# The first row without w_out: gated values through DRAM, output products a row behind

## The chip, the cores and the metric

One core of a Trainium2 chip runs the program. TensorE multiplies matrices, VectorE and ScalarE do elementwise work, POOL (GpSimd) takes a share of it, and SyncE issues all the DMAs. The metric is the device time of one execution in microseconds, the median over runs.

## The reference

Eight items of x (8 heads, 512 rows of 64) and a state of 32 rows a head go through attention in both directions, and then two feed-forward blocks run over 4608 tokens of width 512:

```python
scores = scale * x @ state^T;  xread = softmax(scores) @ state       # 512 rows an item
sread = softmax(scale * state @ x^T) @ x                             # 32 rows an item
t = concat([xread, sread]) as (tokens, 512)
gate = sigmoid(t @ w_gate); val = t @ w_val                          # 512 -> 1536
y = (gate * val) @ w_out                                             # 1536 -> 512
h = y @ w_in; u = h * softmax(h); out = layernorm(u) * g @ w_out2    # 512 -> 1024 -> 512
```

All weights of the feed-forward blocks arrive as 64-bit floats.

## The kernel before

The work goes in rows, one for each item (the eight sread pieces together make one more). A row computes, for 12 column blocks c of 128 of w_gate and w_val: 12 matmuls for gate and value into gps and vps (`first_mm`), the sigmoid of gps into sg (ScalarE, L599), the product with vps into sg (VectorE, L603, called gate product here), the split of sg into a high part gh and a low part gl, and 12 matmuls that add gh and gl times the rows c of w_out into the four sums acc (`out_acc`, called output products, always one column behind). Each fp32 product is three matmuls, high x high, high x low and low x high; a split is one copy for the high part and one subtraction for the low part. xread is never formed: TensorE multiplies the state with the weights first (`state_w1` for the first row, one column at a time, L580; `state_w` for the others, half a pair of columns at a time, L516), the result is split into mh and ml (L131, L137), and `first_mm` multiplies these with the softmax weights ah and al. While row b runs, the attention of item b + 1 is spread over its columns (`parts`).

In the first row the weights are also made from their 64-bit words (class Conv). `load` issues the DMA of 512 KB into a stage, `take` is two ScalarE operations (L197, L198), `form` two bit operations and a sign step on VectorE (L205, L208, L215), `add` an integer addition on POOL (L225), which frees the stage. For w_gate and w_val that ends in wf; for w_out `split` follows (ScalarE copy and POOL subtraction, L234) into woh and wol. So the first row makes three such blocks a column, and in it gl comes from POOL (L609). In the second row `split_w` splits wf into xe and xo (ScalarE and POOL, L504), two pieces a column; the third row's states (`state_w` for item 2, with item 3) need them, six matmuls each.

Inside a row each engine runs its instructions in the order in which the code is written; SyncE issues DMAs in that order too. At the end of a row `y_spill` sends the four sums to DRAM. From the third row on, made states come partly from DRAM: item 3's are stored in msp by `state_w` and loaded by `state_load`, and later ones come from qsp.

## Time and profile before

| | us |
|---|---|
| median of three runs (1111.26 to 1114.22) | 1113.05 |
| the profiled execution | 1113.68 |
| its span | 1111.8 |
| TensorE busy | 1079.4 (97%) |
| VectorE busy | 760.7 (68%) |
| ScalarE busy | 577.1 (52%) |
| POOL busy | 383.5 (34%) |

The span is the time from the first to the last event that the profile shows. The shares are means over rows that have different limits, so the first rows have to be read apart. The profile names lines of the kernel before; the changed kernel's lines are some higher.

### The profile page before, as it was taken

What the parts mean: (1) busy time and instruction counts of PE and PEld (TensorE: products, weight loads), DVE (VectorE), ACT (ScalarE), POOL (GpSimd) and SP (SyncE); (2) the same over time, 40 slices, a digit from 0 to 9 for tenths busy, and PEclk for the clock granted to TensorE, in tenths of its full rate; (3) what the DMA queues carried; (4) which work ended last, traced back from release to release, by engine and by line L of the source; (5) the groups of instructions that cost most, each with busy time, mean ns of one, the idle gap of its engine ahead of it and who ended that gap; (6) DMA issues with size and microseconds to landing.
All of it is one profiled execution on the core that took longest, in us unless ns stands there. A gap on an engine that the chain in (4) does not pass through costs nothing.

```text
span 1111.8 us, 16156 instructions
## 1 busy us (share of the span) xinstructions
PE 1079.4 (97%) x5497; PEld 848.5 (76%) x5497; DVE 760.7 (68%) x1335; ACT 577.1 (52%) x1120; POOL 383.5 (34%) x441
## 2 busy tenths in 40 slices
PE   8877899999999999999999999999999999999998
PEld 6655567777877767778878998877788878888887
DVE  5999956367466556556365367997677777778773
ACT  5766545555444344334344344665556566565553
POOL 2777733310000000000000042216576667677551
PEclk9899999999999999999999999999999999999999
DMA  8764040241274374352341325421543543553441
GB/s 229 238 203 138 1 116 1 68 103 34 62 184 167 127 220 132 102 143 67 89 114 48 125 96 152 114 57 58 161 152 124 168 164 124 176 166 121 153 143 38
DMA packets 148946, 135.62 MB, mean 122 GB/s; under 512 B 74240, under 2 KB 114432, under 8 KB 148864
## 3 DMA queue, kind: packets, MB, share of 16 engines
q1 hardware_dynamic: 148864, 134.60, 40.6%
q8 instruction: 43, 0.70, 0.3%
q14 instruction: 39, 0.32, 0.1%
HBM read 84.74 MB, written 49.81 MB: 121 GB/s over the span
## 4 chain that ended last, share of the span: by engine, by line
PE 74%; DVE 15%; issue 3%; DMA 3%; ACT 2%; SPq 2%; POOL 1%; DVEq 0%; POOLq 0%; ACTq 0%
PE acc L140 10%; PE acc L142 9%; PE acc L141 9%; PE att L142 5%; PE att L140 5%; PE att L141 5%; PE gps L140 4%; PE gps L141 4%; PE gps L142 4%; PE vps L140 4%; PE vps L141 4%; PE vps L142 4%; DVE wf L215 2%; DVE wf L205 2%; DVE wf L208 1%
## 5 line engine op out<-in xcount | busy, mean ns | idle before, releaser
L140 PE MATMUL acc<-gh,woh 128*128 128x512 f32 (+1 forms) x432 | 172.5, 399 | 0.7 <-ACT gh L131 0.7
L141 PE MATMUL acc<-gl,woh 128*128 128x512 f32 (+1 forms) x432 | 166.1, 384 | 1.9 <-POOL gl L609 1.3
L142 PE MATMUL acc<-gh,wol 128*128 128x512 f32 (+1 forms) x432 | 165.5, 383 | 0.0
L603 DVE TENSOR_TENSOR sg<-vps,sg 128x512 f32<-128x512 f32 (+1 forms) x108 | 71.0, 658 | 137.8 <-PE vps L142 118.3
L599 ACT ACTIVATE sg<-gps 128x512 f32<-128x512 f32 (+1 forms) x108 | 61.6, 571 | 150.6 <-PE gps L142 149.0
L140 PEld LDWEIGHTS acc<-gh,woh 128*128 128x128 f32 x432 | 82.4, 191 | 42.1 <-issue 26.1
L258 POOL MEMSET xtr<- 32x256 f32 x14 | 4.2, 303 | 272.1 <-PE att L326 271.7
L141 PEld LDWEIGHTS acc<-gl,woh 128*128 128x128 f32 x432 | 82.4, 191 | 17.4 <-POOL gl L609 2.5
L142 PEld LDWEIGHTS acc<-gh,wol 128*128 128x128 f32 x432 | 82.3, 191 | 16.1
L814 POOL TENSOR_TENSOR wol<-ut,woh 128x512 fp32r<-128x512 f32 x48 | 61.8, 1302 | 90.7 <-ACT woh L131 90.7
L131 ACT ACTIVATE gh<-sg 128x512 fp32r<-128x512 f32 (+1 forms) x101 | 60.6, 600 | 62.1 <-DVE sg L603 62.1
L225 POOL TENSOR_TENSOR tt<-tt,xn 128x512 int32<-128x512 int32 x16 | 23.5, 1471 | 195.0 <-DVE tt L215 172.1
L609 DVE TENSOR_TENSOR gl<-sg,gh 128x512 fp32r<-128x512 f32 (+1 forms) x97 | 68.9, 710 | 17.9 <-ACT gh L131 14.4
L140 PE MATMUL gps<-ah,mh 128*128 128x512 f32 x192 | 76.1, 397 | 4.8 <-DVE ml L137 3.0
L142 PE MATMUL att<-woh,wol 128*128 128x512 f32 (+1 forms) x204 | 79.6, 390 | 0.7 <-POOL wol L814 0.6
L140 PE MATMUL att<-woh,woh 128*128 128x512 f32 (+1 forms) x204 | 79.8, 391 | 0.0
L141 PE MATMUL att<-wol,woh 128*128 128x512 f32 (+1 forms) x204 | 79.3, 389 | 0.0
L140 PE MATMUL vps<-ah,mh 128*128 128x512 f32 x192 | 75.2, 392 | 1.1 <-DVE ml L137 1.1
L141 PE MATMUL gps<-al,mh 128*128 128x512 f32 x192 | 75.4, 393 | 0.7 <-DVE al L137 0.7
L142 PE MATMUL gps<-ah,ml 128*128 128x512 f32 x192 | 75.4, 393 | 0.1
L142 PE MATMUL vps<-ah,ml 128*128 128x512 f32 x192 | 75.2, 392 | 0.0
L141 PE MATMUL vps<-al,mh 128*128 128x512 f32 x192 | 75.0, 391 | 0.0
(464 smaller groups left out, 2762.8 us busy)
## 6 DMA issues: line engine op xcount, KB each, us to landing
usp<-ub SPq DMA_DIRECT2D x32, 512.0 KB, 2.6
ut<-usp SPq DMA_DIRECT2D x128, 128.0 KB, 2.9
qsp<-qst SPq DMA_DIRECT2D x48, 256.0 KB, 2.3
stg<-qsp SPq DMA_DIRECT2D x192, 64.0 KB, 2.0
out_dram<-sg SPq DMA_DIRECT2D x32, 256.0 KB, 3.0
xn<-in_x_dram SPq DMA_DIRECT2D x15, 512.0 KB, 5.2
e2t<-in_x_dram SPq DMA_DIRECT2D x96, 64.0 KB, 2.5
stge<-in_moe_w_out_dram SPq DMA_DIRECT2D x10, 512.0 KB, 3.6
```

Source lines behind the costliest of these rows:

```text
L131: return act(dst, src, AF.Copy)
L140: mm(o, lh, rh, start=start, stop=False, **kw)
L141: mm(o, lh, rl, start=False, stop=False, **kw)
L142: return mm(o, ll, rh, start=False, stop=stop, **kw)
L205: vec.tensor_scalar(out=t, in0=t, scalar1=EXP_LO, scalar2=EXP_HI, op0=ALU.max, op1=ALU.min)
L208: vec.tensor_scalar(out=tu, in0=tu, scalar1=3, scalar2=0x3FFFFFFF, op0=ALU.logical_shift_left, op1=ALU.bitwise_and)
L215: vec.scalar_tensor_tensor(out=tu, in0=hi, scalar=0xC0000000, in1=tu, op0=ALU.bitwise_and, op1=ALU.bitwise_or)
L225: pool.tensor_tensor(out=ti, in0=ti, in1=lo, op=ALU.add)
L599: act(sg[c % 2][:, 0:n], gps[:, 0:n], AF.Sigmoid)
L603: vec.tensor_tensor(out=g, in0=vps[:, 0:n], in1=g, op=ALU.mult)
L609: eng.tensor_tensor(out=gl[c % 2][:, 0:n], in0=sg[c % 2][:, 0:n], in1=r(gh[c % 2][:, 0:n]), op=ALU.subtract)
L814: pool.tensor_tensor(out=lv, in0=wv[:, 4 * q:4 * q + 4], in1=r(hv), op=ALU.subtract)
```

## The change

The first row converts w_gate and w_val only. Its gated values go to DRAM (gsp[0]), column by column; it makes no output products. Instead it makes the states of the second row, from the weights in wf as they become ready, a column later, and sends them to DRAM (msp[1]). The second row loads them, splits them, converts w_out (three stages of its own), reloads the first row's gated values and makes the first row's output products; its own gated values go to DRAM too (gsp[1]). A new loop of 12 columns before the third row reloads those, makes the second row's output products and three states of the third row. The splits of wf go one a column in eight columns of the second row and two a column in eight columns of the new loop. The stages of the first row are eight instead of ten, none of them shared with the spill buffers.

```diff
--- before.py
+++ after.py
@@ -15,7 +15,7 @@
 ALU = mybir.AluOpType
 AX = mybir.AxisListType
 P = 128
-STAGES = 10
+STAGES = 8
 WARM = 11
 EXPS = 7
 QUAD = 4
@@ -104,7 +104,7 @@
 
     early = ExitStack()
     sbe = early.enter_context(tc.tile_pool(name="sbe", bufs=1, side="right"))
-    stg0 = stg + [sbe.tile([P, 1024], F32, name=f"stge{i}") for i in range(STAGES - 2)]
+    stg0 = [sbe.tile([P, 1024], F32, name=f"stge{i}") for i in range(STAGES)]
     cvt0 = [sbe.tile([P, 512], F32, name=f"cvte{i}") for i in range(4)]
     xq1 = [sbe.tile([P, S], F32, name=f"xq{i}") for i in range(4)]
     stf1 = sbe.tile([P, 512], F32, name="stf1")
@@ -117,6 +117,7 @@
     ysp = [tc.dram_tile([KC, P, S if b < B else SR], F32, name=f"ysp{b}") for b in range(B + 1)]
     ssp = tc.dram_tile([B, P, KC * NS], F32, name="ssp")
     qsp = [tc.dram_tile([H, P, 512], F32, name=f"qsp{p}") for p in range(NF1 // 2)]
+    gsp = [[tc.dram_tile([P, 512], F32, name=f"gsp{b}_{c}") for c in range(NF1)] for b in range(2)]
     msp = [tc.dram_tile([NF1, P, 512], F32, name=f"msp{b}") for b in range(B)]
 
     mm = nc.tensor.matmul
@@ -511,11 +512,7 @@
         n = 2 * p + g
         h, l = mh[i % 3], ml[i % 3]
         s = spill[n % 4]
-        if b < 2:
-            for q in range(2):
-                mm(o[64 * q:64 * q + 64, :], stt[b % 2][:, 2 * g + q, :], wpart(wf, p, 2 * g + q), start=True, stop=True)
-            put(o, h, l, hi)
-        elif b < QUAD and b % 2 == 0:
+        if b < QUAD and b % 2 == 0:
 
             for q, o in enumerate((gps, o2)):
                 k = 2 * g + q
@@ -529,6 +526,15 @@
                 nc.sync.dma_start(out=msp[b + 1][n, 64 - 64 * q:128 - 64 * q], in_=s[64 * q:64 * q + 64])
         else:
             put(s, h, l, hi)
+
+    def state_next(n, hi=hi_of):
+
+        p, g = divmod(n, 2)
+        o, s = acc[2], spill[n % 4]
+        for q in range(2):
+            mm(o[64 * q:64 * q + 64, :], stt[1][:, 2 * g + q, :], wpart(wf, p, 2 * g + q), start=True, stop=True)
+        hi(s, o)
+        nc.sync.dma_start(out=msp[1][n], in_=s)
 
     def state_load(b, n):
         if b < QUAD:
@@ -614,6 +620,17 @@
         for m in ms:
             sl = slice(m * P, (m + 1) * P)
             mm3(ps_acc(m, n), h[:, sl], l[:, sl], gh[i][:, 0:n], gl[i][:, 0:n], c == 0, c == NF1 - 1)
+
+
+    def g_store(b, c):
+        nc.sync.dma_start(out=gsp[b][c], in_=sg[c % 2])
+
+    def g_load(b, c, ring):
+        if c < NF1:
+            nc.sync.dma_start(out=ring[c % len(ring)], in_=gsp[b][c])
+
+    def g_split(c, ring, hi=hi_of):
+        put(ring[c % len(ring)], gh[c % 2], gl[c % 2], hi)
 
     def y_spill(b, n, after):
         for m, s in enumerate(xtr + e2t if after == SREAD else [tt[0], ee[0], ee[1], tt[1]]):
@@ -846,10 +863,7 @@
     def rings(n):
         return (n % 2, xn[n % 2]), tt
 
-    jobs = [job(c, t) for c in range(2) for t in range(2)]
-    for c in range(NF1):
-        jobs += [job(c, 2)] + ([job(c + 2, t) for t in range(2)] if c + 2 < NF1 else [])
-    conv = Conv(jobs, rings0)
+    conv = Conv([job(c, t) for c in range(NF1) for t in range(2)], rings0)
 
 
     ring = [(b, p, g) for b in blocks[1:] if b < B for p in range(NF1 // 2) for g in range(2)]
@@ -871,7 +885,7 @@
         loaded = max(loaded, made - NF1)
         while loaded < min(made - NF1 + n, len(ring)):
             b, p, g = ring[loaded]
-            if b < 2 or paired(b) and b % 2 == 0 or b >= QUAD and quads and quads[0] <= (p, 2 * g + 1):
+            if b < 1 or paired(b) and b % 2 == 0 or b >= QUAD and quads and quads[0] <= (p, 2 * g + 1):
                 return
             state_load(b, 2 * p + g)
             loaded += 1
@@ -993,63 +1007,99 @@
                     conv.take()
 
 
-
-        ahead = {4: 3, 5: 3, EXPS: 0}
+        ahead = {EXPS - 2: 2, EXPS - 1: 2, EXPS: 0}
         for c in range(NF1):
-            part = parts[c]
+            pe, others = parts[c]
             if c > 0:
                 first_mm(0, c, 0, 0)
             sigma(c, S)
-            if c == EXPS + 1:
-                conv.split(hi_vec)
-                gated_hi(c - 1, S, hi_vec)
-                gated_lo(c - 1, S)
-                first_mm(0, c, 1, 0)
-                form(2)
-                state_w1(c + 1, att[0])
-                take(1)
-                gated(c, S)
-                out_acc(c - 1, S)
-                form(1)
-                conv.split()
-                gated_hi(c, S)
-                gated_lo(c, S, pool)
-                take(ahead.get(c, 2))
-                part[1]()
-                continue
-            form(2)
+            form(3)
             if c > 0:
                 first_mm(0, c, 1, 0)
             else:
                 state_w1(1, acc[1])
             gated(c, S)
-            take(1)
-            if part[0]:
-                part[0]()
-            if c + 1 == NF1:
-                a_next(blocks[1])
-                make()
-                make(o=vps)
-            elif c > 0:
-                state_w1(c + 1)
+            g_store(0, c)
             if c != EXPS:
-                conv.split()
-            if c == EXPS:
-                part[1]()
+                take(1)
+            if pe:
+                pe()
+            hi = hi_vec if c == EXPS else hi_of
+            if 0 < c < NF1 - 1:
+                state_w1(c + 1, acc[1], hi=hi)
+            if c > 0:
+                state_next(c - 1, hi)
+            take(ahead.get(c, 1))
+            others()
+        state_next(NF1 - 1)
+        a_next(blocks[1])
+        loads(3)
+        make()
+        make()
+    early.close()
+    for p in range(2):
+        x_pool(p)
+    early = ExitStack()
+    sbe = early.enter_context(tc.tile_pool(name="sbe2", bufs=1, side="right"))
+    stg2 = [sbe.tile([P, 1024], F32, name=f"stgf{i}") for i in range(3)]
+    cvt2 = [sbe.tile([P, 512], F32, name=f"cvtf{i}") for i in range(2)]
+    gst = [sbe.tile([P, 512], F32, name=f"gst{i}") for i in range(3)]
+    conv = Conv([job(c, 2) for c in range(NF1)], lambda n: ((n % 3, stg2[n % 3]), cvt2))
+
+    with tc.manual_schedule():
+        parts = attention(2)
+        for _ in range(3):
+            conv.load()
+        for c in range(2):
+            g_load(0, c, gst)
+        conv.step(1)
+        for c in range(NF1):
+            pe, others = parts[c] if c < len(parts) else (None, None)
+            hi = hi_vec if others == exps else hi_of
+            first_mm(1, c, 0, used)
+            sigma(c, S)
+            first_mm(1, c, 1, used)
+            used += 2 * (c % 2)
+            gated(c, S)
+            g_store(1, c)
+            if others == exps:
+                a_cols(1)
+                exps()
+            if c == NF1 - 1:
+                a_next(2)
+            if pe:
+                pe()
+            if made - NF1 < NF1:
+                make(1, hi=hi)
             if c > 0:
                 out_acc(c - 1, S)
-            if c != EXPS:
-                gated_hi(c, S)
-            form(1)
-            if c != EXPS:
-                gated_lo(c, S, pool)
-                take(ahead.get(c, 2))
-                part[1]()
+            g_split(c, gst, hi)
+            g_load(0, c + 2, gst)
+            loads(3)
+            conv.step(1)
+            if others and others != exps:
+                others()
+            if c == 0:
+                load_xq(2, 1)
+            if 2 <= c < 10:
+                split_w(1)
+        for c in range(2):
+            g_load(1, c, sg)
+    assert not conv.jobs and not conv.loaded and not conv.joined
     early.close()
-    for p in range(3):
-        x_pool(p)
+
     with tc.manual_schedule():
-        for n_b, b in enumerate(blocks[1:], 1):
+        for c in range(NF1):
+            make(o2=vps)
+            out_acc((c - 1) % NF1, S)
+            g_split(c, sg)
+            g_load(1, c + 2, sg)
+            if c == 0:
+                y_spill(0, S, 1)
+            if c < 8:
+                split_w(2)
+    with tc.manual_schedule():
+        for n_b, b in enumerate(blocks[2:], 2):
             before = blocks[n_b - 1]
             n_before = S if before < B else SR
             n = S if b < B else SR
@@ -1124,8 +1174,6 @@
                         load_xq(n_b + 1, 1)
                 if nxt == SREAD and c == len(parts):
                     nc.sync.dma_start(out=xn[0][:, 0:KC * SR].rearrange("p (b e) -> p b e", b=B), in_=ssp.rearrange("b p e -> p b e"))
-                if n_b == 1:
-                    split_w(2)
                 if b == SREAD and c == 0:
                     conv = Conv([(rows(w_in2, k, f), win(k, f), None) for k in range(KC) for f in range(2)], rings)
                     conv.load()
```

TensorE in the first row, one column: the last product of gate and value, the states (wf is the converted weights, stt_113 and stt_114 the states of item 0 and 1), and what follows. Before:

```order
L142 MATMUL vps<-ah_90,ml 128x512
L580 MATMUL gps<-wf_145,stt_113 64x256 x4
L140 MATMUL acc_174<-gh_96,woh_68 128x512
L141 MATMUL acc_174<-gl_98,woh_68 128x512
L142 MATMUL acc_174<-gh_96,wol_80 128x512
L140 MATMUL acc_175<-gh_96,woh_68 128x512
```

And in the changed kernel:

```order
L143 MATMUL vps<-ah_90,ml 128x512
L586 MATMUL acc_175<-wf_145,stt_113 64x256 x4
L535 MATMUL acc_176<-wf_149,stt_114 64x512 x2
L141 MATMUL gps<-ah_89,mh 128x512
L142 MATMUL gps<-al_91,mh 128x512
L143 MATMUL gps<-ah_89,ml 128x512
```

The output products (acc, gh, woh) are gone from the column; four matmuls of the second row's states (L535) stand in their place, between the first row's states (L586) and the next product.

SyncE where the first row ends (ssp takes sread, xn and e2t the x of item 2, stg the spilled states). Before:

```order
L427 DMA ssp<-e2t_108 128x128
L263 DMA xn_99<-in_x_dram 128x4x256
L263 DMA xn_100<-in_x_dram 128x4x256
L280 DMA e2t_107<-in_x_dram 32x16x32 x4
L280 DMA e2t_108<-in_x_dram 32x16x32 x4
L625 DMA ysp_184<-tt_103 128x512
```

And in the changed kernel, where msp is the second row's states and gsp the gated values:

```order
L537 DMA msp_225<-stg_112 128x512
L428 DMA ssp<-e2t_108 128x128
L264 DMA xn_99<-in_x_dram 128x4x256
L264 DMA xn_100<-in_x_dram 128x4x256
L281 DMA e2t_107<-in_x_dram 32x16x32 x4
L281 DMA e2t_108<-in_x_dram 32x16x32 x4
L537 DMA msp_225<-stg_112 128x512
L541 DMA stg_111<-msp_225 128x512 x2
L541 DMA stg_112<-msp_225 128x512
L626 DMA gsp_0_212<-sg_109 128x512
```

The loads of the first three states (stg from msp) stand behind the two loads of xn, the eight of e2t and the store of the last state.

POOL in the second row (xo is the low part of wf, wol that of w_out, cvtf its 64-bit conversion). Before:

```order
L504 TENSOR_TENSOR xo_1206<-wf_153,xe_1205 128x512 x4
L504 TENSOR_TENSOR xo_1211<-wf_149,xe_1210 128x512 x4
L504 TENSOR_TENSOR xo_1216<-wf_145,xe_1215 128x512 x4
L504 TENSOR_TENSOR xo_1542<-wf_141,xe_1541 128x512 x4
L504 TENSOR_TENSOR xo_1666<-wf_137,xe_1665 128x512 x2
```

And in the changed kernel, three columns:

```order
L505 TENSOR_TENSOR xo_1025<-wf_153,xe_1024 128x512
L235 TENSOR_TENSOR wol_81<-cvtf_1037,woh_69 128x512
L226 TENSOR_TENSOR cvtf_1038<-cvtf_1038,stgf_1036 128x512
L505 TENSOR_TENSOR xo_1025<-wf_153,xe_1024 128x512
L235 TENSOR_TENSOR wol_82<-cvtf_1038,woh_70 128x512
L226 TENSOR_TENSOR cvtf_1037<-cvtf_1037,stgf_1034 128x512
L505 TENSOR_TENSOR xo_1025<-wf_153,xe_1024 128x512
L235 TENSOR_TENSOR wol_83<-cvtf_1037,woh_71 128x512
L226 TENSOR_TENSOR cvtf_1038<-cvtf_1038,stgf_1035 128x512
```

One piece of wf a column is left there, and the addition and the split of w_out have come in.

## Rows read from the trace of the kernel before

**Rows 1.** The page's 40 slices of 27.8 us: busy tenths of TensorE and VectorE.
```profile
PE   8877899999999999999999999999999999999998
...
DVE  5999956367466556556365367997677777778773
```

**Rows 2.** Windows: us, busy (instructions) PE, PEld, DVE, ACT, POOL, PEclk, DMA share, GB/s.
```profile
30.00:35.00 5.00, 3.94 (x22) 2.17 (x21) 4.97 (x9) 4.73 (x8) 3.31 (x3) 0.94 1.08 365
30.95:141.36 110.41, 91.78 (x520) 63.38 (x521) 107.78 (x158) 71.19 (x131) 81.22 (x59) 0.95 0.43 135
40.00:45.00 5.00, 5.00 (x17) 3.67 (x14) 4.96 (x9) 1.71 (x4) 3.32 (x3) 0.66 0.34 109
141.36:227.05 85.69, 85.69 (x432) 61.23 (x430) 45.90 (x77) 44.90 (x87) 30.82 (x25) 1.00 0.26 61
```

**Rows 3.** Timeline of VectorE, first row and (last) second: start us, us, line, operation, tiles.
```profile
70.49 0.41 DVE L208 TENSOR_SCALAR wf<-wf 128x512 uint32<-128x512 uint32 x1
70.82 0.68 DVE L215 SCALAR_TENSOR_TENSOR cvte<-stge,cvte 128x512 uint32<-128x512 uint32 x1
...
72.03 0.67 DVE L603 TENSOR_TENSOR sg<-vps,sg 128x512 f32<-128x512 f32 x1
...
78.40 1.50 DVE L205 TENSOR_SCALAR wf<-wf 128x512 f32<-128x512 f32 x1
...
81.69 0.68 DVE L603 TENSOR_TENSOR sg<-vps,sg 128x512 f32<-128x512 f32 x1
...
96.11 0.68 DVE L349 TENSOR_TENSOR tt<-tt,smm 128x512 f32<-128x512 f32 x1
...
97.49 0.73 DVE L205 TENSOR_SCALAR cvte<-cvte 128x512 f32<-128x512 f32 x1
...
146.57 0.69 DVE L137 TENSOR_TENSOR ml<-gps,mh 128x512 fp32r<-128x512 f32 x1 [1.53 <-ACT mh L131]
```

**Rows 4.** Timeline of POOL, first row and (last) second row.
```profile
71.63 1.63 POOL L225 TENSOR_TENSOR cvte<-cvte,stge 128x512 int32<-128x512 int32 x1 [1.69 <-DVE cvte L215]
...
78.15 1.47 POOL L609 TENSOR_TENSOR gl<-sg,gh 128x512 fp32r<-128x512 f32 x1
...
149.46 2.56 POOL L504 TENSOR_TENSOR xo<-wf,xe 128x512 fp32r<-128x512 f32 x2 [7.00 <-ACT xe L131]
```

**Rows 5.** Timeline of TensorE, after a wait in the first row, and in the second.
```profile
39.19 1.08 PE L580 MATMUL gps<-wf,stt 128*64 128x256 f32 x8 [1.95 <-POOL wf L225]
...
40.60 0.62 PE L141 MATMUL acc<-gl,woh 128*128 128x512 f32 x1
...
44.01 0.51 PE L140 MATMUL acc<-gh,woh 128*128 128x512 f32 x1
...
180.47 1.08 PE L516 MATMUL gps<-wf,stt 128*64 128x512 f32 x4
181.47 0.50 PE L140 MATMUL acc<-gh,woh 128*128 128x512 f32 x1
...
184.34 0.39 PE L140 MATMUL gps<-ah,mh 128*128 128x512 f32 x1
...
187.15 1.08 PE L516 MATMUL gps<-wf,stt 128*64 128x512 f32 x4
```

**Rows 6.** Timeline of ScalarE in the second row, the high half of a state product.
```profile
145.94 0.60 ACT L131 ACTIVATE mh<-gps 128x512 fp32r<-128x512 f32 x1 [2.36 <-PE gps L516]
```

**Rows 7.** Timeline of SyncE, issues of DMAs.
```profile
141.17 0.94 SPq L263 DMA_DIRECT2D xn<-in_x_dram  x2
142.21 5.85 SPq L280 DMA_DIRECT2D e2t<-in_x_dram  x8
...
302.44 1.31 SPq L535 DMA_DIRECT2D stg<-msp  x3
```

**Rows 8.** Instructions on the tensor msp: its transfers from issue to landing.
```profile
DMA to landing us min/median/max: 2.2/2.3/5.6
```

**Rows 9.** DMA issues by line, 15 to 40 us: KB each, median us to landing.
```profile
stg<-in_moe_w_gate_dram SPq DMA_DIRECT2D x1, 512.0 KB, 8.5
```

## The prediction

> **What bounds the kernel now.** I read the page's slices first: in the second to fifth, VectorE is at nine tenths and TensorE at seven or eight; from the sixth on TensorE is at nine [rows 1]. Then the windows, cut where the program changes rows. From 30.95 us (the weights by states for column 1) to 141.36 us (the second row's first product) VectorE works 107.8 of 110.4 us and POOL 81.2; in the second row, to 227.05 us, TensorE works all of 85.69 and VectorE 45.9 [rows 2]. So the first row is set by converting weights, and the second by TensorE.
>
> One column step of the first row shows how. Gate products stand 9.66 us apart, at 72.03 and 81.69. A bit operation issues every 0.33 us and the sign step every 0.6 [rows 3], but the one at 78.40 takes 1.50, because POOL is in an operation from 78.15 to 79.62 [rows 4]. The gate product at 72.03, which reads one operand in PSUM, runs in 0.67 beside POOL's addition of 71.63. So bit operations, and VectorE operations with both operands in SBUF, wait for POOL and POOL for them. Such work of one step: POOL 5 x 1.28 (two in 2.56) = 6.4; VectorE 3 conversions x (2 x 0.33 + 0.6) = 3.8 [rows 3, 4]; together 10.2 in a step of 9.66.
>
> The Trainium skill (SBUF — State Buffer, "SBUF: two separate sides") calls this pair of ports an exclusive lock held for the whole instruction. The step agrees nearly: 10.2 us of locked work pass in 9.66. As a mere sum, the second row after the change would hold 71.7 us of locked work by the rule and 67.8 by that ratio; both are below the 72.2 that TensorE needs there (below), which would give 1110. I go by the order of the operations instead.
>
> How much TensorE waits in the first row: a plain step of the second row is 6.68 us [rows 5]: 1.00 for four state matmuls, 2.87 for the 12 output matmuls, 2.81 for the 12 of gate and value. Attention is what is left of 85.69 - 12 x 2.81 - 12 x 2.87 - 10 x 1.00 - 2 x 1.4 (states of row three: six matmuls of 0.23) = 4.8 a row. The first row then holds 11 x 2.81 + 11 x 2.87 + 13 x 1.00 + 7.0 of attention (the next row's 4.8, and 2.2 that I estimate for the half which item 0 still owes) = 82.5 of 110.4. **The prize is 28 us**, if the rest hides.
>
> **The change, part by part.** TensorE's instructions are kept; they change places. Times count from the profiled execution's start.
>
> *First row, step by step.* The 12 conversions, splits and output products of w_out leave; four state matmuls a step for the second row come in. TensorE has 2.81 + 1.00 + 1.00 = 4.81 a step. The new chain, state matmuls to mh to ml to the next product, has to fit in the second group of state matmuls: mh takes 0.60 on ScalarE and ml starts 0.63 after it began [rows 3, 6], so the product can start 0.75 after the states end, under the 1.00. VectorE has 2 x 1.27 + gate product 0.6 + ml 0.6 + attention of some 1.3 (an estimate: 45.9 of the second row less 38 operations of 0.68, a twelfth of it, less its waits for POOL) = 5.0: level with TensorE. Column 1's product starts 2.0 after 30.95 (states 1.0, mh 0.6, and starts), at 32.9, as before. From there to column 11's: 10 x 4.81 = 48.1, attention 6.1 (0.7 comes before or after), then 2.81: the row would end at 89.9.
> What is late: columns 6 and 7 convert three weights instead of two, so ml comes 0.7 and 1.1 late. At the exponentials' column VectorE is in series: after ml the subtraction, maximum and scale 1.4 (96.11 to 97.49 before) [rows 3], six bit operations and three sign steps 3.8, 1.9 of POOL's three additions of the step before that fall on locked operations, gate product 0.6, and the high half, now on VectorE, 0.6: 8.3 against TensorE's 3.8, which ends at the first states. Product 8 starts 10.0 after product 7, 5.2 late. After an idle 1.95 us before 39.19 the granted clock is 0.66 of full from 40 to 45: eight matmuls from 40.60 to 44.01 start 0.43 apart instead of 0.23, at the lower level of 1.2 GHz [rows 2, 5]. I add 2.1 for such a restart. The first row's last product ends at 89.9 + 1.8 + 5.2 + 2.1 = **99.0** (bounds 93, if the exponentials' step goes as the others, and 108, rival one).
> The stores of gated values and states cost nothing here: 2 x 0.52 + 2 x 0.26 = 1.57 MB a step is 4.3 us at the 365 GB/s of rows 2, in a step of 4.8 to 6. The queue is a rival below.
>
> *The boundary.* Before, the second row's states came off TensorE; now they come from DRAM, and their loads stand on SyncE behind the x of row three (second piece in the section on the change). Counted from the end of the last product: spill of state 10 stored at 2.0 + 0.45, ssp 0.4, xn 0.94, eight x pieces 5.85 [rows 7]. Before, nothing that TensorE needed stood behind those eight. Then the store of state 11, 0.5 (three loads issue in 1.31, rows 7), the first load landing 2.3 after issue [rows 8], mh 0.6 and the matmul's start: 13.8 in all, of which TensorE works 2.4. Nothing else is ready for it, since output products wait for the next loop. The second row starts at **112.8** (111 if the x pieces issue at xn's 0.47 each, 116 if the load takes the 5.6 of rows 8), and at the lower clock: 2.1 more.
>
> *Second row.* TensorE loses its state matmuls: 12 x 2.81 + 11 x 2.87 + 4.8 = 70.1, + 2.1 clock = 72.2. w_out's conversion moves here. POOL: 12 splits, 11 additions, 8 splits of gate and value = 31 x 1.28 = 39.7. VectorE, locked: ml 10 x 0.6 and gl 12 x 0.6, which now read SBUF on both sides, conversions 11 x 1.27, attention about 4.8 (estimated from its subtractions and products) = 32.0. That 71.7 is level with TensorE's 72.2 is why order decides. Walking the steps with each engine's order and alternating the lock: at column 1 the scores wait for transposes that stand behind ml, gl and a conversion, 2.0; at column 3, 0.5; from column 4 on wol or gl arrives 0.4 to 1.2 after the output product could start, some 2.3 together. **77.0** (72.2 with no wait at all, 84 with two and a half times these).
>
> *The new loop.* 12 x 2.87 + three states of row three 3 x 1.4 = 38.6. Each reload of a gated value must land within two steps of 2.8: gl is done 2.4 into a step (0.6 + 0.6 and one POOL operation), issue 0.4, 2.3 to land, so 5.1 of 5.6. POOL's two splits a step (2.56) can hold gl back by one operation. I take 1.5 for this and the spill of four sums: **40.1** (38.6 to 46). It makes three states where before two were ahead, so row three is 1.4 shorter.
>
> *Unchanged or nothing:* the start to 30.95 (eight stages instead of ten: the same first six loads are issued ahead of x; w_out's were waited for by nobody there); from row three on the instructions are the same.
>
> *Sum.* 99.0 + 13.8 + 77.0 + 40.1 - 1.4 = 228.5, against 227.05: **+1.4 us**. The profiled execution took 1113.68 (span 1111.8 and 1.9 around it), the median of the runs is 1113.05. 1113.68 + 1.4 = 1115.1; I say 1115. Of the prize, the first row's own waits keep 9.6, the boundary takes 11.4 and 2.1, the second row 4.8, the loop 1.5: 29.4.
>
> **The rivals.** *One: the gated stores hold the first row (slower).* A store of gated values is issued behind two weight loads that wait for POOL's additions, some 3 us after the product, and the sigmoid two columns later writes the same buffer. By the walk it must land within about 7 us of its issue. 512 KB loads in a full queue took up to 8.5 [rows 9]; with two such loads ahead of it a store at 9 us delays gate product, ml and the next product by 2, in five of the ten steps: +10, 1125. Against it: 1.57 MB need 4.3 us of the step, so the queue should drain.
> *Two: the lock lets more pass than I walk (faster).* Locked work passed at 10.2 in 9.66; if VectorE and POOL overlap a little in every pair, the second row runs at TensorE's 72.2 (-4.8), columns 6 to 8 of the first lose 3 of their 7: -8, 1107. Against it: the 1.50 of rows 3 is a full wait.
> *Three: everything hides (faster).* Only the boundary and its clock remain, 13.5 of 28: -14.5, 1099. Against it: VectorE and TensorE are level in both rows, and no slack is left for attention's uneven steps.
>
> **How the numbers follow.** About 0.3%, or 3.3 us, is what a measurement here can tell from no change. Forecast, 0.45: faster 0.06, same 0.29, slower 0.10; its own range 1108 to 1121. Rival one, 0.25: slower 0.25. Rival two, 0.23: faster 0.20, same 0.03. Rival three, 0.07: faster. Together faster 0.33, same 0.32, slower 0.35. The range reaches into both sides, from 1102 (below it rival three) to 1126 (above it the worse half of rival one).
>
> **What would show it.** Gate products in the first row 5 to 6.5 us apart, save one of about 10; the last near 99. TensorE idle for about 10 us near 102, released by a load of states, and a lower clock after it. In the second row waits of TensorE for POOL's wol and VectorE's gl of about 1 us each, with POOL near 40 us busy; 12 steps of about 2.9 after it. Wrong if the first row's steps stay above 7 (ended by a DMA: rival one), or if TensorE is busy through the second row (rival two), or if the wait at the boundary is under 6.

## The result and the profile after

The changed kernel takes 1119.55 us (median of 1117.92 to 1120.16), the kernel before 1112.65 beside it: ratio 1.0059, interval 1.0042 to 1.0077, or 4.7 to 8.6 us slower. The forecast was +1.4 (1115.0, own range 1108 to 1121). The time lies in that range; the size of the loss does not follow from the sum, which had called it no change. The profiled execution has a span of 1118.4, 6.6 more than before.

The page's slices after the change, against [rows 1]:
```profile
PE   7976789999999999999999999999999999999998
...
DVE  6975799457556556556365367997577778778773
POOL 2541256610000000000000042216566667676551
PEclk9989899999999999999999999999999999999999
```
VectorE, full in the second to fifth slice before, is now full in the second, sixth and seventh: the second row carries w_out's conversion. TensorE has a hole in the fourth (6, from 84 to 112 us); from the seventh on it reads as before.

The windows, cut where the prediction's terms end, against [rows 2] (columns: the window and its length, busy us and instructions of PE, PEld, DVE, ACT, POOL, granted clock, DMA share, GB/s):
```profile
30.01:99.65 69.64, 62.20 (x406) 37.74 (x407) 56.75 (x114) 46.98 (x86) 32.37 (x25) 0.95 0.71 233
```
```profile
...
99.65:115.92 16.27, 2.48 (x12) 0.54 (x10) 2.59 (x6) 3.34 (x8) 0.00 (x0) 0.71 0.87 248
115.92:195.00 79.08, 73.11 (x366) 55.93 (x367) 71.63 (x104) 50.21 (x96) 43.55 (x32) 0.97 0.61 182
195.00:242.37 47.37, 46.31 (x205) 37.32 (x205) 23.03 (x30) 27.06 (x48) 24.01 (x17) 1.00 0.46 132
```
The first is the first row, from column 1's product to the end of the last; the second the boundary; the third the second row; the fourth the loop and row three up to its gate product 1 (at 237.74 before, where the same stretch, from 227.05, took 10.69). The boundary's 16.27 us with 2.48 of TensorE is the longest single loss.

| us | forecast | measured | difference |
|---|---|---|---|
| start, to column 1's product | 32.9 | 30.0 | -2.9 |
| first row | 66.1 | 69.6 | +3.5 |
| boundary | 13.8 | 16.3 | +2.5 |
| second row | 77.0 | 79.1 | +2.1 |
| loop and row three to gate product 1 (40.1 - 1.4 + 10.69) | 49.4 | 47.4 | -2.0 |
| from there to the end (874.1 before: span less 237.74) | 874.1 | 876.0 | +2.0 |

The differences sum to +5.2, which is the measured 6.6 less the forecast 1.4. Two of them are scatter: among eleven traces of the changed kernel and of its versions below that have the same code up to there, the first gate product stands between 30.57 and 36.27 us, and in two traces of the kernel before at 33.58 and 33.10; the stretch behind row three's gate product 1 varies from 873 to 877. So the first row's end (99.65) came near the forecast 99.0 by two errors that cancel: the row was 3.5 longer, and started 2.9 earlier in this execution. From gate product 0 of row one to gate product 1 of row three, which leaves both out, it is 204.2 before (204.2 again in the second trace) and 211.7 after: **+7.5**.

The boundary, first on SyncE, where the loads stand in issue order, against [rows 7]:
```profile
102.89 1.02 SPq L264 DMA_DIRECT2D xn<-in_x_dram  x2
104.01 6.28 SPq L281 DMA_DIRECT2D e2t<-in_x_dram  x8
110.38 0.43 SPq L537 DMA_DIRECT2D msp<-stg  x1
110.86 1.40 SPq L541 DMA_DIRECT2D stg<-msp  x3
```
then on ScalarE and TensorE (in brackets the idle time before and what ended it):
```profile
103.36 1.14 ACT L132 ACTIVATE ah<-ee 128x512 fp32r<-128x512 f32 x2
115.23 1.22 ACT L132 ACTIVATE mh<-stg 128x512 fp32r<-128x512 f32 x2 [10.73 <-DMA stg<-msp]
```
```profile
101.74 1.08 PE L535 MATMUL acc<-wf,stt 128*64 128x512 f32 x4 [0.70 <-ACT stg L132]
115.92 0.79 PE L141 MATMUL gps<-ah,mh 128*128 128x512 f32 x1 [13.10 <-ACT mh L132]
```
The new row's scores were split at 104.5; everything after that waits for three state loads that SyncE issues behind x. The first is used 4.4 us after its issue, where 2.3 [rows 8] was assumed. A matmul of 0.79 shows the lower clock behind the idle.

The exponentials' column on VectorE, against the 1.4 of [rows 3]:
```profile
67.18 0.68 DVE L350 TENSOR_TENSOR tt<-tt,smm 128x512 f32<-128x512 f32 x1
67.78 0.68 DVE L369 TENSOR_REDUCE st<-att 128x1 f32<-128x512 f32 x1
68.49 0.15 DVE L370 TENSOR_SCALAR st<-st 128x1 f32<-128x1 f32 x1
68.56 2.54 DVE L206 TENSOR_SCALAR wf<-wf 128x512 f32<-128x512 f32 x3
71.02 1.08 DVE L209 TENSOR_SCALAR wf<-wf 128x512 uint32<-128x512 uint32 x3
72.03 2.97 DVE L216 SCALAR_TENSOR_TENSOR wf<-stge,wf 128x512 uint32<-128x512 uint32 x3
74.92 0.68 DVE L609 TENSOR_TENSOR sg<-vps,sg 128x512 f32<-128x512 f32 x1
75.52 0.68 DVE L135 CAST mh<-acc 128x512 fp32r<-128x512 f32 x1
```
```profile
76.34 0.76 PE L141 MATMUL gps<-ah,mh 128*128 128x512 f32 x1 [4.61 <-DVE mh L135]
```
This is the forecast's series in its order: product 8 starts 10.9 after product 7 (10.0 forecast), 6.4 of it three conversions (5.7 forecast). TensorE then works at the lower level: 0.57 of full from 75 to 80.

The second row's waits of TensorE, 116 to 195 us (us in total, times, longest):
```profile
...
PE vps L141 <- DVE sg L609: 1.7, 1, 1.7
PE att L327 <- DVE xtr L323: 1.6, 1, 1.6
PE gps L143 <- DVE ml L138: 1.4, 1, 1.4
PE acc L143 <- POOL wol L235: 1.2, 2, 0.6
```
Left out is the boundary's 13.1. These sum to 5.9 against 4.8, and only 1.2 is wol's. VectorE and POOL do stand in each other's way here:
```profile
127.73 1.79 DVE L138 TENSOR_TENSOR gl<-gst,gh 128x512 fp32r<-128x512 f32 x1
```
```profile
127.47 1.50 POOL L235 TENSOR_TENSOR wol<-cvtf,woh 128x512 fp32r<-128x512 f32 x1 [0.95 <-ACT woh L132]
```
A subtraction of 0.68 takes 1.79 and ends 0.55 after POOL's, as if it had begun when POOL let go. That agrees with what the Trainium skill (SBUF — State Buffer, "SBUF: two separate sides") states of the port pair that the two share: the operation that starts first has it, as an exclusive lock, for the whole instruction.

### The profile page after: what moved, and what is told of

It reads as the page before. It is cut to its first block, busy times and chain, and to the rows that moved or that the text cites. A ratio compares the mean times of both kernels' runs of the same rounds, so it can differ in the third digit from the quotient of the medians.

```text
span 1118.4 us, 16344 instructions
## 1 busy us (share of the span) xinstructions
PE 1073.3 (96%) x5497; PEld 844.1 (75%) x5497; DVE 756.2 (68%) x1346; ACT 584.5 (52%) x1132; POOL 368.3 (33%) x430
## 4 chain that ended last, share of the span: by engine, by line
PE 68%; DVE 13%; DMA 8%; issue 4%; ACT 3%; SPq 3%; POOL 2%; DVEq 0%; POOLq 0%; ACTq 0%
PE acc L141 10%; PE acc L142 9%; PE acc L143 9%; PE att L143 4%; PE att L141 4%; PE att L142 4%; PE gps L141 4%; PE gps L143 4%; PE gps L142 4%; PE vps L141 4%; PE vps L142 3%; PE vps L143 3%; DMA usp<-ub 2%; POOL tt L226 2%; PE gps L569 1%
## 5 line engine op out<-in xcount | busy, mean ns | idle before, releaser
L141 PE MATMUL acc<-gh,woh 128*128 128x512 f32 (+1 forms) x432 | 168.9, 391 | 0.8 <-ACT gh L132 0.8
L142 PE MATMUL acc<-gl,woh 128*128 128x512 f32 (+1 forms) x432 | 163.7, 379 | 1.3 <-DVE gl L138 1.1
L141 PEld LDWEIGHTS acc<-gh,woh 128*128 128x128 f32 x432 | 81.3, 188 | 30.8 <-issue 13.8
L132 ACT ACTIVATE gh<-sg 128x512 fp32r<-128x512 f32 (+1 forms) x91 | 54.6, 600 | 76.4 <-DVE sg L609 61.9
L141 PE MATMUL att<-woh,woh 128*128 128x512 f32 (+1 forms) x204 | 79.9, 392 | 1.4 <-ACT woh L132 1.4
L615 DVE TENSOR_TENSOR gl<-sg,gh 128x512 fp32r<-128x512 f32 (+1 forms) x84 | 58.7, 699 | 19.8 <-ACT gh L132 16.4
```

Source lines behind the costliest of these rows:

```text
L132: return act(dst, src, AF.Copy)
L141: mm(o, lh, rh, start=start, stop=False, **kw)
L142: mm(o, lh, rl, start=False, stop=False, **kw)
L615: eng.tensor_tensor(out=gl[c % 2][:, 0:n], in0=sg[c % 2][:, 0:n], in1=r(gh[c % 2][:, 0:n]), op=ALU.subtract)
```

## The experiments

All are versions of the changed kernel. Times are given as ratios to the kernel before, run beside them (the changed kernel: 1.0059). The stages come from VectorE's timeline, by the starts of the gate products (sg<-vps,sg), one trace each: first row from gate product 0 to 11, then to the second row's 0, to its 11, and to row three's 1. A traced execution need not be a typical one: that of "splits late" took 1123.86 us (median 1117.24), that of "one bit operation" 1108.96 (median 1113.26), and the sums do not rank as the ratios do.

| run | ratio (interval) | first row | boundary | second row | loop | sum |
|---|---|---|---|---|---|---|
| before | 1 | 103.2 | 7.6 | 78.8 | 14.6 | 204.2 |
| changed | 1.0059 (1.0042 to 1.0077) | 69.6 | 20.7 | 72.5 | 49.0 | 211.7 |
| loads first | 1.0014 (1.0001 to 1.0026) | 68.2 | 12.3 | 74.6 | 48.9 | 204.1 |
| column, first try | 1.0096 (1.0076 to 1.0117) | 72.1 | 21.7 | 74.0 | 48.9 | 216.8 |
| splits late | 1.0052 (1.0034 to 1.0070) | 69.4 | 20.7 | 69.0 | 54.0 | 213.1 |
| states in row two | 0.9984 (0.9969 to 0.9998) | 71.3 | 6.1 | 80.0 | 48.5 | 205.9 |
| column, second try | 1.0043 (1.0026 to 1.0060) | 68.2 | 20.8 | 71.9 | 49.0 | 210.0 |
| combined | 1.0006 (0.9993 to 1.0019) | 68.0 | 10.2 | 76.0 | 52.1 | 206.2 |
| combined, splits in row three | 1.0015 (0.9999 to 1.0032) | 67.8 | 10.6 | 69.9 | 56.2 | 204.5 |
| x early | 1.0026 (1.0010 to 1.0043) | 69.5 | 10.2 | 77.0 | 49.2 | 205.9 |
| x early, splits in row three | 1.0013 (1.0000 to 1.0025) | 69.4 | 11.6 | 70.2 | 52.1 | 203.2 |
| one bit operation | 1.0021 (1.0006 to 1.0037) | 62.0 | 21.1 | 72.1 | 49.0 | 204.1 |
| states in row two, column | 0.9981 (0.9972 to 0.9990) | 66.3 | 6.1 | 79.9 | 48.5 | 200.8 |

**The state loads ahead of x.**
```diff
-            (a_sread_t_mm, lambda: [a_sread_t_copy(1), load_row(2)]),
+            (a_sread_t_mm, lambda: a_sread_t_copy(1)),
...
         loads(3)
+        load_row(2)
```


> The x of row three (two xn loads, eight pieces) is issued behind the first three loads of the second row's states instead of ahead of them. Theory (the boundary is a queue on SyncE): the first state load issues at about 103.3 us instead of 110.9, the second row's first product starts at 108 instead of 115.9, TensorE's idle time there falls from 13.1 to about 5.5, and the kernel takes about 1112 (-7.5). Rival (the wait only moves: the transposes of row three's x, or the reloads of gated values behind x, hold the second row's first columns instead): -2 to 0. A landing time of 4.2 us as in the changed kernel, with less in the queue ahead, would fall to about 2.3.

Measured 4.5 per mille below the changed kernel (5 us). Its SyncE and its TensorE at the boundary:
```profile
103.86 1.42 SPq L541 DMA_DIRECT2D stg<-msp  x3
105.38 0.93 SPq L264 DMA_DIRECT2D xn<-in_x_dram  x2
106.36 8.24 SPq L281 DMA_DIRECT2D e2t<-in_x_dram  x8
```
```profile
107.48 0.79 PE L141 MATMUL gps<-ah,mh 128*128 128x512 f32 x1 [4.66 <-ACT mh L132]
```
The load issues at 103.86 as forecast, is used 2.9 us later (ScalarE's mh at 106.80) and idle falls from 13.1 to 4.7. So the queue order is shown as the cause of 8.4 us there. The rival holds in part: the second row grows by 2.1, with two waits for x's transposes (3.3 in all).

**The states made in the second row**, as before: that part of the change undone.
```diff
...
+        if b < 2:
+            for q in range(2):
+                mm(o[64 * q:64 * q + 64, :], stt[b % 2][:, 2 * g + q, :], wpart(wf, p, 2 * g + q), start=True, stop=True)
+            put(o, h, l, hi)
...
-            if c > 0:
-                state_next(c - 1, hi)
...
-        state_next(NF1 - 1)
         a_next(blocks[1])
-        loads(3)
         make()
-        make()
+        make(o=vps)
```


> The second row's weights by states are made in the second row again, as in the kernel before (no store and reload of them); everything else as in the changed kernel. Theory (the round trip costs the boundary; the first row is set by VectorE): idle at the boundary falls from 13.1 to about 4 and the clock stays up (-10), the second row gains ten times 1.0 of TensorE but loses part of its 5.9 of waits (+7), the first row gains 2 to 3 in steps where TensorE was level: -5, 1114.5. Rival A (the first row is set by TensorE, so its steps shorten by 1.0 each): first row -10, total 1107. Rival B (the second row's waits add to the new TensorE work): -1 to +1, 1119.

Measured 7.5 per mille below the changed kernel, just below the kernel before. The table shows the trade: making the states early saves 7.5 in the second row (80.0 to 72.5) and costs 14.6 at the boundary (6.1 to 20.7). The first row did not shorten when 1.0 of TensorE left each of its columns (71.3), so rival A falls. That does not show that VectorE sets the row. TensorE now waits for mh in front of ten products, and a plain step, from one product to the next, is as long as before, 5.00:
```profile
49.17 0.50 PE L141 MATMUL gps<-ah,mh 128*128 128x512 f32 x1 [0.70 <-ACT mh L132]
...
54.17 0.50 PE L141 MATMUL gps<-ah,mh 128*128 128x512 f32 x1 [0.70 <-ACT mh L132]
```
for 4.97 in the changed kernel, where the products are followed by both groups of state matmuls:
```profile
48.31 0.50 PE L141 MATMUL gps<-ah,mh 128*128 128x512 f32 x1
...
51.41 1.08 PE L586 MATMUL acc<-wf,stt 128*64 128x256 f32 x8
...
53.28 0.50 PE L141 MATMUL gps<-ah,mh 128*128 128x512 f32 x1
```
The four matmuls L535 had filled the time that the chain from the first row's states over mh to the next product takes in any case: 0.75 in the prediction, 0.70 here. The granted clock, 0.89 over the row for 0.95, took some more.

**The exponentials' column**, first try.
```diff
-        ahead = {EXPS - 2: 2, EXPS - 1: 2, EXPS: 0}
+        ahead = {EXPS - 3: 2, EXPS - 2: 2, EXPS - 1: 0, EXPS: 0}
...
-            if c != EXPS:
+            if c not in (EXPS - 1, EXPS):
                 take(1)
```


> First row: no weights are converted in the exponentials' column (7) nor in 8; three each are converted in columns 5 and 6, two in 9 and 10. Theory (column 7 is long because VectorE does six bit operations and three sign steps there between the exponentials' maximum and the gate product): product 8 starts 6 us after product 7 instead of 10.9, columns 5 and 6 grow by 0.5 to 1 together, in all -4, 1115.5. Rival (column 7 is set by ScalarE's four exponentials, not by conversions): product 8 stays 9 or more after product 7, 0 to -1.

Measured 3.7 per mille above the changed kernel. Product 8 still came 9.2 after product 7 (68.59 and 77.74 us), and TensorE then waited for weights (us, times, longest), at the states of columns 9 and 10:
```profile
...
PE acc L586 <- POOL wf L226: 5.5, 3, 3.1
```
That is a fault of my distribution (5.0 of the 5.5 stand at 88.89 and 98.13 us): these weights were converted in the column that uses them. The run says nothing of the theory beyond the 9.2.

**The column, second try:** two weights of ScalarE's part are taken again at the column's end.
```diff
             others()
+            if c == EXPS:
+                take(2)
```


> The exponentials' column again, with the weights not made late: three converted in columns 5 and 6, none in 7, two in 8 and 9 (their ScalarE part is taken at the end of column 7, behind the exponentials). In the run before this one product 8 came 5.1 us after product 7, but TensorE then waited 5.5 us for converted weights in columns 9 and 10. Theory (the exponentials' column costs about 5 because conversions stand in it): product 8 stays at 5 to 6 us, no wait for weights over 1 us, first row 4 us shorter, the kernel 4 us below the changed kernel (1.002 of before). Rival (VectorE's work in the first row is a sum, and a conversion moved is only paid in another column): gate product 0 to gate product 11 still 69 to 70 us, no gain.

The 5.1 in this expectation was misread: it is the distance of two gate products, one column on; the products stood 9.2 apart. Here they stand 9.1 apart (69.33 and 78.47; 10.9 in the changed kernel), where the theory had 5 to 6. The wait of 4.6 in front of product 8 is gone, but product 7 now waits 2.4 for its ml, behind the three conversions of column 6, and the states after it 1.6 for a weight from POOL:
```profile
72.42 0.50 PE L143 MATMUL gps<-ah,ml 128*128 128x512 f32 x1 [2.37 <-DVE ml L138]
```
By gate products, the steps from 4 to 6 take 13.7 instead of 12.2 and the one from 6 to 7 takes 4.9 instead of 8.9. The first row is 1.3 shorter and the kernel 1.6 per mille, within the two intervals. The rival is nearer: most of the work is paid in another column.

**One bit operation left out.**
```diff
-            for _, _, _, _, t, _, _ in jobs:
+            for _, _, _, _, t, dst, _ in jobs:
+                if not isinstance(dst, tuple):
+                    continue
                 tu = t.bitcast(U32)
```


> The conversion of the gate and value weights (and of w_in2 near the end) leaves out the second of its two bit operations on VectorE, so these weights are other numbers; everything else as in the changed kernel. That takes 0.43 us twice a column from VectorE and nothing from TensorE, ScalarE or POOL. Theory (the first row's step is a sum of VectorE's work, since taking 1.0 us a column from TensorE left it at 70 us): gate product 0 to 11 falls by 6 to 9 from 69.6, the kernel 6 to 8 below the changed one. Rival (the step is a chain through all engines, state matmuls, mh, ml, product, in which conversions stand beside): -2 or less, save 1 in the exponentials' column.

The first row falls by 7.6 (VectorE's busy time by 8.1), which is the theory's number; the kernel by 3.8 per mille (4 us), less than 6 to 8. The windows of the first row, the changed kernel's and this one's:
```profile
30.69:100.27 69.58, 62.14 (x409) 37.78 (x410) 56.69 (x114) 46.30 (x85) 31.69 (x25) 0.95 0.71 232
```
```profile
30.11:92.06 61.95, 59.26 (x409) 35.94 (x410) 48.57 (x96) 46.64 (x85) 30.56 (x24) 1.00 0.80 267
```
The same 409 matmuls take 59.3 at the full clock and 62.1 at 0.95: the lower clock behind the exponentials' idle costs 2.9 in the changed kernel. The rest of the 7.6 is waits, 7.4 there and 2.7 here: in front of product 8 TensorE waits 1.4 instead of 4.6, and for ml 1.2 instead of 2.7.
```profile
47.72 0.50 PE L141 MATMUL gps<-ah,mh 128*128 128x512 f32 x1
...
52.72 0.50 PE L141 MATMUL gps<-ah,mh 128*128 128x512 f32 x1
...
71.50 0.47 PE L141 MATMUL gps<-ah,mh 128*128 128x512 f32 x1 [1.40 <-DVE mh L135]
```
The plain steps did not shorten (5.00 for 4.97), and seven of the ten steps from product 1 to 11 agree within 0.1 with the changed kernel's. Those from product 5 (7.0 to 5.9), 7 (10.9 to 7.8) and 8, which in the changed kernel runs at the lower clock (7.6 to 5.0), did. So the theory's number came without its mechanism: the step is not a sum of VectorE's work. The rival, a chain beside which the conversions stand, fits seven steps of ten, but gave the exponentials' column 1 where it and the clock behind it gave 5.7.

**The splits moved to the loop.**
```diff
-            if 2 <= c < 10:
-                split_w(1)
...
-            make(o2=vps)
+            if c >= 4:
+                make(o2=vps)
...
-            if c < 8:
-                split_w(2)
+            split_w(2)
```


> The eight splits of the gate and value weights that the second row does on POOL (columns 2 to 9) move to the loop behind it, which then does two in each of its twelve columns; row three's first three states are made from column 4 of that loop on. Theory (VectorE's and POOL's locked work holds the second row): POOL loses 10 us there, TensorE's waits for wol, gate product and ml (4.2 of 5.9) go, the second row takes 75 instead of 79.1, the loop stays within 1 of its time: -3 to -4, 1116. Rival (the waits come from the order of operations on VectorE, not from the lock): 0 to -1.

The second row falls by 3.4, and the loop pays 5.0 (it then waits 3.3 for gl). The ratio can't be told from the changed kernel's. The splits (copies on ScalarE, subtractions on POOL) do hold the second row; taking them away there only moves the time.

**Combined:** the column's second try, and at the boundary:
```diff
-... rows_norm(1), rows_back(), load_states(2)]),
+... rows_norm(1), rows_back(), loads(1), load_states(2), loads(2)]),
...
+            if c == NF1 - 1:
+                a_next(blocks[1])
...
-        state_next(NF1 - 1)
-        a_next(blocks[1])
-        loads(3)
-        make()
-        make()
+        make()
+        make()
+        state_next(NF1 - 1)
+        loads(3)
+        load_row(2)
...
-        parts = attention(2)
+        parts = [(None, lambda: None)] + attention(2)
```


> The column as in the run beside this one, and the boundary rebuilt: the first two state loads are issued in column 10, the second row's scores are split into high and low halves right behind the last product, its first two states before the spill of state 11, row three's x is loaded behind all of it, and row three's attention begins one column later in the second row. Theory (13 us of wait plus clock at the boundary are queue order, and nothing in the chip requires them): TensorE idle at the boundary under 2.5, no lower clock behind it, no wait for the transposes of x over 1; 10 to 12 below the changed kernel from the boundary and 4 from the column: 0.992 of before, about 1103. Rival (the wait goes to the second row, where VectorE and POOL are level with TensorE): the second row grows from 72.5 (gate product 0 to 11) to 76 or more, 0.997 of before.

Measured 1.0006: no gain over the loads alone that the intervals tell. The boundary worked, the second row's first matmul following the first row's last in 4.4 us instead of 16.3:
```profile
103.86 0.50 PE L141 MATMUL gps<-ah,mh 128*128 128x512 f32 x1 [1.28 <-ACT mh L132]
...
106.11 0.50 PE L141 MATMUL gps<-ah,mh 128*128 128x512 f32 x1 [1.03 <-ACT mh L132]
```
but the rival decided (second row 76.0), by another road than it named, on SyncE and ScalarE:
```profile
110.63 9.71 SPq L281 DMA_DIRECT2D e2t<-in_x_dram  x8
120.44 0.43 SPq L626 DMA_DIRECT2D gsp<-sg  x1
```
```profile
122.98 0.60 ACT L605 ACTIVATE sg<-gps 128x512 f32<-128x512 f32 x1 [4.98 <-DMA gsp<-sg]
```
The store of gated values now stands behind x, and a sigmoid waits for it: the mechanism of the prediction's rival one, in the other row. The loop is 3.1 longer too: TensorE waits 2.3 there for the spill of sums, which ScalarE copies late, as shown in the next run.

**Combined, the splits in row three:** as above, with eight splits in the loop and sixteen in row three, where POOL is free (a pool of buffers that row three opens is opened eight columns later).
```diff
-            if 2 <= c < 10:
-                split_w(1)
...
+            if c >= 6:
+                make(o2=vps)
...
+                if n_b == 2 and c < 8:
+                    split_w(2)
```


> As the combined version, and the 24 splits of gate and value weights on POOL leave the second row: eight in the loop behind it, sixteen in row three's first eight columns, where POOL worked 0.6 of 100 us. Theory (locked work of VectorE and POOL holds the second row and the loop): waits of the second row for wol, gate product and ml fall by 3.4, as they did when the splits went to the loop, and the loop, with eight splits instead of sixteen, loses 2 (its waits for gl); row three stays at TensorE's pace: 4 to 5 below the combined version. Rival (row three's VectorE, at 58 of 100 us, then shares the lock with POOL for 20 us and delays TensorE there): 0 to -2.

The second row fell by 6.1, the loop rose by 4.1; no gain in the time. That was neither theory nor rival: row three kept its pace, and TensorE waited 3.5 in the loop for the spill of sums. That was not for the spill's buffers, as an expectation below has it: ScalarE's copy of the sums stands behind the split of a reloaded gated value, and the reload on SyncE behind the next x.
```profile
179.41 6.04 SPq L281 DMA_DIRECT2D e2t<-in_x_dram  x8
...
186.03 5.01 SPq L630 DMA_DIRECT2D sg<-gsp  x3
```
```profile
189.34 0.63 ACT L132 ACTIVATE gh<-sg 128x512 fp32r<-128x512 f32 x1 [7.21 <-DMA sg<-gsp]
```
It is the boundary's mechanism, one row on.

**x early:** the combined boundary, with x in buffers of its own and attention in its old columns.
```diff
+    xq2 = [sbe.tile([P, S], F32, name=f"xt3{i}") for i in range(2)]
...
         parts = attention(2)
+        load_xq(2, 0)
```


> As the combined version, but row three's eight x pieces go into two buffers of their own and are issued in the first row's columns 9 and 10, where SyncE has room, and attention stays in its columns (the ring of reloaded gated values is two deep instead of three to make the space). In the combined version the boundary's idle fell to 3.0 us in all, but the eight pieces then held SyncE from 110.6 to 120.3 and with it the store of gated values: a sigmoid waited 5.0 us for it, the transposes of x 2.9. Theory (each of the waits is the queue on SyncE, and x is what fills it): boundary as in the combined version, second row 72.5 from gate product 0 to 11, no wait for x or gated stores over 1: gate product 0 of row one to gate product 1 of row three 199 to 201 us (211.7 in the changed kernel, 204.2 in the one before), 0.995 of before. Rival (the pieces delay the gated stores of columns 9 and 10 or the first state loads instead): boundary idle over 6, 0.999 to 1.001.

The rival in kind: the x pieces and three loads of w_out's rows now stand ahead of the state loads.
```profile
93.71 2.63 SPq L281 DMA_DIRECT2D xt<-in_x_dram  x5
...
97.52 1.51 SPq L182 DMA_DIRECT2D stgf<-in_moe_w_out_dram  x3
...
100.75 0.54 SPq L542 DMA_DIRECT2D stg<-msp  x1
```
The load issued at 100.75 is used at 107.86, 7.1 later, and the transposes of x hold TensorE for 4.6. The idle at the boundary is 5.2 where the rival had over 6, and the time is above the rival's 1.001.

**x early, the splits in row three.** The two edits above together.

> As the run beside it, and the 24 splits of gate and value weights leave the second row, eight to the loop behind it and sixteen to row three's first eight columns. Theory (POOL's locked work holds the second row; in the run that had this before, the loop was long because its spill of sums waited 3.5 us for buffers that the later attention still held): second row 70, loop no longer than without it, 2 to 3 below the run beside it. Rival (the loop is long whatever the spill: its first states of row three come late, from column 6 on, and row three starts late): second row 70, loop +6, in all 1 to 4 above the run beside it.

1.3 per mille below the run beside it, second row 70.2, loop +2.9: between the two; the intervals overlap.

**The kernel before, again.** Unchanged.

> The kernel before, unchanged, for its trace alone: the first gate product stood at 33.58 us in the first trace of it, and at 30.6 to 33.6 in five traces of versions of the changed kernel. Theory (the start scatters by when the first loads land, and is no effect of the change): a first gate product that differs from 33.58 by 1 to 3 us. Rival (it belongs to the kernel): 33.4 to 33.8. In the stretch behind 760 us TensorE waited 0 for woh then, and 0.8 to 1.6 in five traces of versions of the changed kernel: 0 again if that is an effect of the change.

The first gate product stood at 33.10, so the start scatters little here; the eleven traces named above spread over 6 us on both sides of it. Behind 760 us it had no wait for woh again, and every version of the changed kernel had one of 0.8 to 1.7. Just ahead of that place one load of ut, a tensor of the second block, was issued 4.2 us after its store in the changed kernel and 2.6 before. Why is open; it is about 1 us.

**States in row two, and the column.** The two edits with a gain and no queue in their way.

> The two edits that gained most with the least moved: the second row's weights by states made in the second row (0.9984 of before by itself), and the conversions taken out of the exponentials' column (0.0016 below the changed kernel by itself). Theory (the first adds no queue at the boundary, and the second takes VectorE work out of a serial stretch of the first row): the two add up, 0.996 to 0.998 of before, about 1108 to 1109, first row from gate product 0 to 11 at 70 instead of 71.3. Rival (without the state matmuls of the second row TensorE waits 0.7 for mh in ten steps of the first row, and the exponentials' column is hidden by that): 0.998 to 0.999.

0.9981, interval 0.9972 to 0.9990: faster than both kernels, by 1 to 3 us against the one before. Its first row fell to 66.3 in the trace, but the time can't be told from that of the states alone (0.9984), so that the gains add is not shown. The rival's waits for mh are there (ten, 7.5 in all), and the plain steps are 5.00 again. (Its start, 36.27, was the latest of all.)

## Why the prediction came out as it did

*Start.* Taken as fixed at 30.95; it scatters by some us from trace to trace, which one trace of before could not tell.

*First row.* The forecast was 59.1 of TensorE (57.0 and 2.1 of clock) and 7.0 of waits (1.8 and 5.2). Measured: 62.2 and 7.4. The waits, walked step by step, were right in sum, and the exponentials' series was right in its order. The TensorE term was 3.1 too small: at the full clock the work is 59.3 where I had 57.0, and the clock cost 2.9, not 2.1. Attention, an estimate, was not the reason (6.3 by the starts of its matmuls, for 6.1). The price of the twelve products was: 2.81 comes from the second row, where they stand behind output products; behind state matmuls they take 3.10 (48.31 to 51.41). The eight state matmuls take 1.87 for 2.00, so that a plain step of TensorE is 4.97 instead of 4.81. "VectorE level with TensorE" is not what the experiments show of the plain steps: these keep their length when 1.0 leaves TensorE (the chain over mh is then seen as a wait) and when 0.43 leaves VectorE twice. VectorE's work shows where it comes late, in steps 5 and 7, and in the clock behind the latter. What the exponentials' column waits, 4.6, comes back only in part when its conversions move (the row is 1.3 shorter in the trace of the second try). What would shorten a plain step was not tried.

*Boundary.* The mechanism was right in every link: ssp, xn, eight x pieces, the store, the load, mh. It was mis-sized at two: 2.3 from issue to landing was the median of twelve loads between 302 and 366 us; behind the loads of x it was 4.4 from issue to use (2.9 with x behind it). The x pieces took 6.28 for 5.85. Together 2.5. I had this as 13.8 of which most is queue order, and the experiment confirms the order.

*Second row.* TensorE 73.1 for 72.2, waits 5.9 for 4.8. The kind of wait was half right: the transposes of x were forecast (1.6 for 2.0) and wol (1.2, where 2.3 was for wol and gl), but a gate product (1.7) and an ml (1.4) were not. VectorE makes both. POOL was busy 43.6 (40 forecast).

*Loop.* 2.0 shorter than forecast: the wait, for gl, was 1.1 of the 1.5, and TensorE's work in the stretch 46.3 where the sum has 47.9 (38.6 - 1.4 + 10.69); twelve output matmuls took 2.77 there (201.86 to 204.63) for 2.87.

*Rivals.* One: a single sigmoid of the first row waited for a store, 1.7 us at 56.86, where five products were to lose 2 each; the mechanism bites harder where x stands ahead in the queue, in the combined version. Two: TensorE waits 5.9 in the second row, so no. Three left nothing but the boundary and its clock: TensorE waited 7.4 in the first row and 5.9 in the second besides, so no. What failed as a judgement is the sum's small +1.4: three terms of it were each 2 to 3.5 low, the first row in its products and clock, the boundary in the landing, the second row in waits and TensorE's work, and only the loop was high.

The gain expected of the change went like this: of the 34 us that the first row got shorter (103.2 to 69.6), the output products came back in the loop and row three (+34.4), the second row gave 6.3, and the boundary took 13.1. With the boundary of before that sum would be 5.6 below it, which no version reached: each that kept the early states and shortened the boundary (to 10.2 to 12.3) gave some of it back in the second row (74.6 to 77) or the loop (52.1 and 56.2). With the states left in the second row the change is worth about 2 (0.9984; 0.2 to 3.4 by the interval).

## What to carry to other kernels

Where work is moved across a stage's edge by way of DRAM, list the DMA queue in issue order at that edge: what was harmless there (eight small pieces of the next input) becomes the critical path when something needed at once is issued behind it. Price a reload by its issue behind the queue plus a landing read behind as many loads, and add the lower clock that follows the idle. Price a group of matmuls from a row where the same kind stands ahead of it. Before valuing freed time on one engine, compare the steps one by one and not only the stage: here 1.0 us a column taken off TensorE came back as a wait for mh, and 0.43 twice a column off VectorE shortened the first row by 7.6, but in three steps of ten.

## What the runs showed of the hardware

Eight x pieces of 64 KB took SyncE 5.85 us in the kernel before, 6.28 in the changed one, 8.24 with the state loads first and 9.71 in the combined version; 1.33, 1.93, 2.70 and 2.81 of it went to one issue of the eight. The DMA share in these stretches was 0.98, 0.96, 0.85 and 0.69, so busier DMA engines do not explain it, and the reason is open. The same 256 KB load was used 2.9, 4.4 and 7.1 us after its issue: with no load of x ahead of it, with ten, and with eight and three loads of w_out. The same 409 matmuls took 59.3 us at a granted clock of 1.00 and 62.1 at 0.95, after one idle of 4.6 us; in the run at 1.00 the idle at that place was 1.4. Twelve matmuls of gate and value took 2.81 us behind output products (184.34 to 187.15 in [rows 5]) and 3.10 behind state matmuls, at the full clock.
